# A recurrence with weight conversion beside it: one list of conversions becomes two, with a start step each

## The chip, the cores and the metric

The kernel runs on one core of a Trainium2 chip. The metric is device time in microseconds (us). The core has five engines that run side by side, each through its own instructions in a fixed order: PE (matrix products and transposes; its weight loads are shown as PEld), DVE (vector operations), ACT (scalar operations, copies out of PSUM, lookups), POOL (vector operations on SBUF) and SP (here the issue of nearly all DMAs). An instruction that waits holds up all that stand behind it on its engine.

## The reference, cut to what matters

Three parts follow one another. All data are float32; B = 4 batches, H = 8 heads, S = 768 steps of time, D = 40.

```python
# 1. recurrence: one 40 x 40 state per batch and head
for t in range(S):
    y[:, :, t] = einsum('bhd,bhde->bhe', r_t, state)
    Sa = einsum('bhde,bhe->bhd', state, a_t)
    state = state * w_t[:, :, None, :] - outer(Sa, b_t) + outer(v_t, k_t)
x = y.transpose(0, 2, 1, 3).reshape(B, S, 320)
# 2. gated layer: w_in 320 x 1024, w_out 1024 x 320
h = maximum(x @ w_in, 0)
conv = 3-tap convolution of h over time, weights conv_w per column
x = (h * sigmoid(conv)) @ w_out
# 3. Fourier transform over time and columns, norm, second layer: w_ch1, w_ch2
u = x + real(fft(fft(x, axis=1), axis=2))
out = u + maximum(norm(u) @ w_ch1, 0) @ w_ch2
```

The weights and conv_w reach the kernel as 64-bit floating-point numbers, seen as pairs of 32-bit integers.

## The kernel before, in words

**The recurrence in chunks.** Time is cut into 12 chunks of 64 steps. A block is one chunk of one batch, so there are 48 blocks, and `Attn.run` (L542) works through them in steps: step n handles block n first of all, and the three blocks ahead of it in later stages. `step` (L470) lists the stages, each ended by a yield, seven in a full step: `stage_u` (PE products from the chunk's inverse, then ACT's scaling at L390), `stage_s` (the state's increment: PE, DVE's mask at L414 and L418, POOL's addition and decay at L419 and L420), `stage_y` (the output: PE at L442 and L445 with gt, which DVE made), `stage_ut`, `stage_h` (the next chunk's right-hand side from the state), `stage_g` (PE at L428, then DVE makes gt at L432) and `stage_o` (transposes, DVE's xo at L463, the store). Early and late steps have fewer yields: steps 45 and 46 have six and five.

**Work for later blocks.** `ahead` (L526) prepares blocks 15 to 17 steps before they are used: loads, decays (scans on DVE, products such as L161 on POOL), the gram products at L203 and transposes at L239 on PE. It has nothing left to do from step 33 on. Each group of eight blocks needs the inverse of its triangular matrices. `inverse` (L292) makes it on DVE in 60 operations that depend on one another (L317 and L320) and some transposes, and then merges the parts with 256 small matmuls on PE (L344, L357) and copies on ACT. The inversion of the last group begins about step 33 and has to be merged by step 40.

**The conversion beside it.** Products on PE take the weights as float32 split into a rounded high part and a remainder. `prep` (L684) turns the 64-bit numbers into these in pieces: 12 of w_in, 16 of w_out, 15 of w_ch1 and 20 of w_ch2, in this order, in one list `self.pieces`. A piece is a load of `raw` (issued by SP at L719), two ACT operations (L729, L730), two on DVE (L732, L734), an integer addition on POOL (L736), four empty yields, and a DVE operation that joins the parts (L739). w_out needs the result alone, one store; the other weights are then rounded on ACT (L703) and subtracted on DVE (L706), with two stores. Each part ends with a yield: 8 calls for a piece of w_out, 9 for one of the others, and 1 more for the first load. All the DVE operations of it write or read the tile `pm`. Converted weights lie in DRAM until they are loaded for use. `conv_w` (L710) converts the convolution's weights, 9 calls.

`body` (L1323) gives `att.run` a chain of `prep` down to `NLEFT = 33` pieces left (all of w_in and w_out and two pieces of w_ch1) and `conv_w`: 264 calls. At each yield of a step `run` adds `SIDE = 1.2` to a counter and makes a call for each whole unit. The instructions of a call are placed, on ACT and DVE, behind the last marked instruction of the recurrence (`issue_after`, with `self.mark` and `self.markd`); other than that the order on each engine, SP's too, is made by a scheduler that takes, in program order, what is ready by its own clock. The 33 pieces left are converted later, beside the gated layer.

**The handover.** When the recurrence's instructions are all placed, the gated layer loads its weights (`moe1_start`, L767: w_in by L752 to L756, w_out by L764) and the first x (L789 to L791), which ACT and POOL split at L792 to L797. Its first product with w_in is `hp` at L655; its first with w_out is `acc` at L848, three units later. SBUF tiles of the two parts share room: the conversion's tiles (raw twice, pm twice, py twice, wh, wl: 2 x 2048 + 2 x 1024 + 2 x 1024 + 1024 + 1024 = 10,240 bytes a partition) stand at the right-hand end, where w_out's tile (8 x 320 x 4 = 10,240 bytes) is put next, and a load waits for the last use of what it overwrites.

Of the kernel before, what the change touches and what calls it, by code (L numbers as in the profile page):

```python
# [33 lines left out]
ND = 1  # L34
NF = 1
NLEFT = 33
W1P = 2
W2P = 5
L4 = 2
# [24 lines left out]
GS = 1  # L64
MG = 1
RI = 0.8
SIDE = 1.2
NA = 7
OT = 0
LG = 15  # L70
# [10 lines left out]
class Attn:  # L81
# [457 lines left out]
            self.gram_x(*divmod(m, B))  # L539
            yield  # L540

    def run(self, side):  # L542
        nc, tc = self.nc, self.tc
        self.start()
        wm = self.pst("warm")
        for _ in range(WARM):
            nc.tensor.matmul(wm[:, 0:396], self.ends[:, 0:128], self.ends, start=True, stop=True)
        self.load_pre(0, 0)
        nc.sync.dma_start(self.mdiag, self.i["mdiag"])
        self.load_pre(0, 1)  # L550
        nc.sync.dma_start(self.mltq, self.i["mlt"])
        nc.sync.dma_start(self.ident, self.i["ident"])
        self.load_pre(1, 0)
        self.grp_start(0)
        self.decay(0, 0)
        for hb in range(2):
            if hb:
                self.decay(0, 1)
            for bl in range(2):
                self.gram(0, 2 * hb + bl)  # L560
        for hb in range(2):
            self.load_v(0, hb)
        self.pads()
        for hb in range(2):
            self.load_z(0, hb)
            self.load_r(0, hb)
        inv = self.inverse(0)
        for n in range(ST0):
            next(inv)
        for hb in range(2):  # L570
            for bl in range(2):
                self.gram_x(0, 2 * hb + bl)
        with tc.issue_after(self.late.ins):
            for hb in range(2):
                self.squares(0, hb)
                if hb == 0:
                    self.load_pre(1, 1)
        self.grp_start(1)

        def half(hb):  # L580
            if hb < ST2:
                self.decay(1, hb)
            else:
                with tc.issue_after(self.first.ins):
                    self.decay(1, hb)
            self.squares(1, hb)
            for bl in range(2):
                self.gram(1, 2 * hb + bl)
                self.gram_x(1, 2 * hb + bl)
        half(0)  # L590
        for b in range(B):
            self.stage_h(0, b)
        if ST1:
            half(1)
        next(inv)
        next(inv)
        tr = self.last
        for _ in inv:
            pass
        if not ST1:  # L600
            half(1)
        live, g = [], 1
        for hb in range(2):
            self.load_v(1, hb)
        for k in range(8 - LD, 8 - LG, 2):
            h = divmod((k + LD) // 2, 2)
            self.load_pre(*h)
            with tc.issue_after(tr.ins):
                self.decay(*h)
            self.squares(*h)  # L610
        sd, na = 0.0, 8 - LG
        for n in range(B * NCH + 4):
            while live and n == live[0]["end"]:
                for _ in live.pop(0)["inv"]:
                    pass
            while g <= NCH // 2 and na + LG >= 8 * g and len(live) < 2:
                end = 8 * g - 8 if g > 1 else 4
                live.append(dict(inv=self.inverse(g), end=end, last=0, acc=0.0,
                                 rate=RI * (35 if g == 1 else 70) / 7 / max(1, end - n - MG)))
                next(live[-1]["inv"])  # L620
                g += 1
            pre = []
            for _ in range(1 + (n < NA)):
                if na <= n:
                    pre.append(self.ahead(na))
                    na += 1
            pre = itertools.chain(*pre)
            ag = -GS
            for _ in self.step(n):
                sd += SIDE  # L630
                while sd > 0:
                    with ExitStack() as st:
                        for m in [self.mark, self.markd][:1 + SM]:
                            if m is not None:
                                st.enter_context(self.tc.issue_after(m.ins))
                        next(side, None)
                    sd -= 1.0
                ag += 1.0
                if ag > 0:
                    next(pre, None)  # L640
                for k, v in enumerate(live):
                    v["acc"] += v["rate"]
                    while v["acc"] > 0 and not (v["last"] == "t" and k or v["last"] == "merge" and n < v["end"] - MG):
                        v["last"] = next(v["inv"], None)
                        v["acc"] -= 1.0
            for _ in pre:
                pass
        for _ in side:
            pass


def passes(nc, out, ops):
# [14 lines left out]
class Moe:  # L667
# [382 lines left out]
    def load_w1(self, pool):  # L1050
        w, q = FF2 // W1P, len(self.w1)
        self.w1.append(self.k320(pool, f"w_ch1_{q}", w))
        self.load_k320(self.w1[q], "w_ch1", slice(w * q, w * q + w))
# [6 lines left out]
    def moe2_rest(self, pool):  # L1060
        for _ in range(1, W1P):
            self.load_w1(pool)
        for _ in range(1, W2P):
            self.load_w2(pool)
        self.rows = pool.tile([128, 3 * B], I32, name="rows")
        self.nc.sync.dma_start(self.rows, self.i["rows"])

    def moe2(self, tp):
# [4 lines left out]
        def g3(i):  # L1073
            b, hf, f = units[i]
            q, r = divmod(f, NF2 // W1P)
            fs = slice(128 * r, 128 * r + 128)
# [246 lines left out]
def body(tc, ins, out):  # L1323
    nc = tc.nc
    with tc.tile_pool(name="dram", bufs=1, space=DRAM) as dr, tc.tile_pool(name="flag", bufs=1) as fp:
        xd = dr.tile([B, NG * P3, S], F32, name="xd")

        xh = [dr.tile([B, NG * P3, (NCH // 2 + 1) * C], F32, name=f"xd{hf}") for hf in range(2)]
        flag = fp.tile([1, 1], I32, name="flag")
        moe = Moe(tc, ins, out)  # L1330
        with ExitStack() as ctx:
            tp = ctx.enter_context(tc.tile_pool(name="prep", bufs=1, side="right"))
            att = Attn(ctx, tc, ins, [(xh[0], 0), (xh[1], NCH // 2 - 1)])
            moe.prep_start(dr, fp)
            att.run(itertools.chain(moe.prep(tp, NLEFT), moe.conv_w(tp)))
            att.in_range(flag)
        moe.run([(xh[0], 0), (xh[1], (NCH // 2 - 1) * C)])
        ok = nc.values_load(flag, min_val=0, max_val=1)
        with tc.If(ok < 1):
            General(tc, ins, xd).run()  # L1340
            moe.run([(xd, 0)] * 2)
# [21 lines left out]
```

## Time and profile before

| | |
|---|---|
| median of 3 runs | 995.05 us (995.01 to 995.82) |
| profiled execution, its own time | 997.03 us |
| its span, first to last instruction | 995.3 us |
| mean granted TensorE clock | 0.937 of full speed |
| PE busy | 906.7 us, 91% |
| DVE busy | 684.1 us, 69% |
| ACT busy | 520.7 us, 52% |
| POOL busy | 456.5 us, 46% |

Busy time is what an engine spent in instructions; matmuls are pipelined, so a busy PE is not PE at its peak. The granted clock is the share of TensorE's full 2.4 GHz that the chip allowed; its lower level is 1.2 GHz. Shares over the whole span mix stages with different limits, and the change lies in one of them, the recurrence, which fills the first half of the span; so the rows further down are by stretch.

### The profile page before, as it was taken

Reading aid. Unit: us, or ns where it says so; the run is one execution under the profiler, and the core shown is the slowest. Engines: PE = TensorE matmul, PEld = TensorE weight load, DVE = VectorE, ACT = ScalarE, POOL = GpSimd, SP = SyncE. Lnnn points to the kernel's source line nnn. Section 1 sums busy time; section 2 is a strip of 40 time slices with the busy share of each in tenths; the row PEclk is TensorE's granted clock in tenths of the full one; section 3 lists DMA queues with packets and bytes.
Section 4 is the critical chain, followed back from the end, with each engine's and each line's share of the span. In section 5 each row is a group of like instructions: output and inputs, shape, how many; then the busy total and the mean of one; then the engine's idle time right before and its main releaser. Section 6 shows DMA issues by size and latency. Waiting matters only on the chain. (4 is left out here: it accounts for less than half of the span.)

```text
span 995.3 us, 21859 instructions
## 1 busy us (share of the span) xinstructions
PE 906.7 (91%) x8178; PEld 818.7 (82%) x8178; DVE 684.1 (69%) x1322; ACT 520.7 (52%) x1448; POOL 456.5 (46%) x528
## 2 busy tenths in 40 slices
PE   5568698999989999999999699989999999999997
PEld 3557587888878888998888587777879999999997
DVE  8895997997996996881278697879684535424321
ACT  5668387676766577334376566567464431212211
POOL 6575375665665464343168566765562121101000
PEclk8667599997997999999999899998999999999999
DMA  9624346565555364339344643112105000000000
GB/s 224 178 77 128 90 126 178 154 161 147 150 138 152 98 169 114 87 98 255 81 126 134 187 141 114 54 50 70 41 1 172 20 1 21 20 20 21 20 14 31
DMA packets 102878, 101.15 MB, mean 102 GB/s; under 512 B 47160, under 2 KB 89003, under 8 KB 102763
## 3 DMA queue, kind: packets, MB, share of 16 engines
q1 hardware_dynamic: 100795, 94.73, 34.3%
q0 software_dynamic: 1968, 4.93, 1.6%
q8 instruction: 67, 1.10, 0.5%
q14 instruction: 48, 0.39, 0.2%
HBM read 74.81 MB, written 20.76 MB: 96 GB/s over the span
## 5 line engine op out<-in xcount | busy, mean ns | idle before, releaser
L831 DVE SCALAR_TENSOR_TENSOR c<-h,cw,c 128x384 f32<-128x384 f32 x128 | 113.3, 890 | 21.0 <-ACT c L829 17.4
L1085 DVE SCALAR_TENSOR_TENSOR gl<-hp,gh 128x384 fp32r<-128x384 f32 x80 | 44.4, 557 | 111.3 <-ACT gh L1084 111.2
L848 PE MATMUL acc<-w_out_f,z 128*128 128x320 f32 x384 | 118.0, 446 | 2.8 <-POOL z L837 1.1
L1084 ACT ACTIVATE gh<-hp 128x384 fp32r<-128x384 f32 x80 | 39.3, 492 | 149.8 <-PE hp L655 149.6
L848 PEld LDWEIGHTS acc<-w_out_f,z 128*128 128x128 f32 x384 | 73.5, 196 | 27.0 <-ACT x L853 1.8
L655 PE MATMUL hp<-xh,w_in_h 128*128 128x386 f32 x192 | 76.3, 397 | 14.3 <-ACT h L822 14.3
L655 PE MATMUL hp<-uh,w_ch_h 128*128 128x384 f32 x240 | 82.3, 343 | 0.0
L655 PE MATMUL hp<-ul,w_ch_h 128*128 128x384 f32 x240 | 81.0, 337 | 0.0
L1108 POOL DMA_INDIRECT out<-o,rows x12 | 11.7, 978 | 150.8 <-DVE o L1103 131.9
L317 DVE TENSOR_TENSOR tmp<-A 128x30 f32<-128x30 f32 (+9 forms) x150 | 77.1, 514 | 3.3
L320 DVE TENSOR_TENSOR A<-A,tmp 128x30 f32<-128x30 f32 (+9 forms) x150 | 76.8, 512 | 3.5
L203 PE MATMUL gram<-abd,kb 120*128 120x192 f32 (+1 forms) x288 | 64.6, 371 | 13.4 <-DMA w<-in_w 6.9
L419 POOL TENSOR_TENSOR st<-st,sm 120x360 f32<-120x360 f32 x40 | 48.3, 1208 | 56.9 <-DVE sm L418 53.0
L1098 PE MATMUL acc<-w_ch_h,gh 128*128 128x320 f32 x240 | 73.2, 312 | 0.0
L1098 PE MATMUL acc<-w_ch_l,gh 128*128 128x320 f32 x240 | 73.0, 309 | 0.0
L203 PEld LDWEIGHTS gram<-abd,kb 120*128 120x128 f32 x288 | 56.0, 227 | 17.3 <-POOL lk L223 9.7
L655 PE MATMUL hp<-xl,w_in_h 128*128 128x386 f32 x192 | 67.1, 349 | 0.0
L736 POOL TENSOR_TENSOR pm<-pm,py 128x160 int32<-128x160 int32 (+2 forms) x64 | 45.0, 703 | 44.0 <-DVE pm L734 17.1
L832 ACT ACTIVATE c<-c 128x384 f32<-128x384 f32 x64 | 33.4, 522 | 60.5 <-DVE c L831 60.3
L161 POOL TENSOR_TENSOR kb<-kb,vx 120x768 f32<-120x768 f32 x24 | 44.0, 1833 | 45.5 <-DMA kb<-in_kb 25.3
L445 PE MATMUL yp<-x,gt 128*64 128x40 f32 x768 | 54.8, 233 | 10.1 <-DVE gt L432 10.1
L445 PEld LDWEIGHTS yp<-x,gt 128*64 128x64 f32 x768 | 51.0, 143 | 13.2 <-DVE gt L432 11.9
(226 smaller groups left out, 2585.9 us busy)
## 6 DMA issues: line engine op xcount, KB each, us to landing
kb<-in_kb SPq DMA_DIRECT2D x24, 360.0 KB
vbd<-in_vbd SPq DMA_DIRECT2D x24, 320.0 KB
xd<-xo SPq DMA_DIRECT2D x56, 90.0 KB
w<-in_w SPq DMA_DIRECT2D x24, 185.6 KB
a<-in_a SPq DMA_DIRECT2D x24, 180.0 KB
z<-in_zv SPq DMA_DIRECT2D x24, 180.0 KB
zt<-in_vt SPq DMA_DIRECT2D x24, 180.0 KB
rbd<-in_r SPq DMA_DIRECT2D x72, 60.0 KB
```

Source lines behind the costliest of these rows:

```text
L161: self.markp = nc.gpsimd.tensor_tensor(kb, kb, vx[:, :, 2:66].unsqueeze(2).to_broadcast([P3, 6, 2, C]), op=ALU.mult)
L203: nc.tensor.matmul(gp[:, 192 * gi:192 * gi + 64 * nh], d["kb"][:, bl * NG + gi].rearrange("p a b -> p (a b)"), abd[:, 0:nh, bl * NG + gi], ...
L317: nc.vector.tensor_tensor(tmp, A[:, s + 1:32, s:s + 1].to_broadcast([128, n, s]), A[:, s:s + 1, 0:s].to_broadcast([128, n, s]), op=ALU.mult)
L320: nc.vector.tensor_tensor(A[:, s + 1:32, 0:s], A[:, s + 1:32, 0:s], tmp, op=ALU.add)
L419: nc.gpsimd.tensor_tensor(self.st[b], self.st[b], t, op=ALU.add)
L445: nc.tensor.matmul(yp[0:64, D * h:D * h + D], gt[:, h], d["x"][:, bl, D * h:D * h + D], start=(c == 0), stop=True, skip_group_check=True)
L655: nc.tensor.matmul(out, l, r, start=(j == 0), stop=(j == len(ops) - 1))
L736: nc.gpsimd.tensor_tensor(m, m, y, op=ALU.add)
L831: nc.vector.scalar_tensor_tensor(c, h[:, j:HS + j], cw[:, f, j:j + 1], c, op0=ALU.mult, op1=ALU.add)
L848: nc.tensor.matmul(self.acc[t][:, 0:DM], z[:, ts], w[:, f], start=(f == 0), stop=(f == NF1 - 1))
L1085: nc.vector.scalar_tensor_tensor(gl, hp[:, 0:HS], 0.0, gh.bitcast(F32), op0=ALU.max, op1=ALU.subtract)
L1098: nc.tensor.matmul(self.acc[t][:, 0:DM], l[:, ts], r, start=(f == 0 and j == 0), stop=(f == NF2 - 1 and j == 2))
```

## The change

The chain handed to `run` becomes two lists, each with the step from which it is taken. The first starts at step `N1ST = 4` and stops at `NLEFT + NW = 49` pieces left: it holds the 12 pieces of w_in, two of w_out, and then conv_w. The second starts at step `N2ND = 38` and goes down to 33 pieces left: 14 of w_out and two of w_ch1. `SIDE` becomes a pair: no calls before step 4, 1.2 for each yield from step 4, 2.2 from step 38. A call goes to the first list that isn't at its end. What is not done when the steps are over is still placed behind them. The pieces, their instructions and their order are as before, and so is the conversion beside the gated layer.

```diff
+NW = 16
+N1ST, N2ND = 4, 38
...
-SIDE = 1.2
+SIDE = (1.2, 2.2)
...
-    def run(self, side):
+    def run(self, sides):
...
+            k = sum(n >= m for m, _ in sides) - 1
             for _ in self.step(n):
-                sd += SIDE
+                sd += SIDE[k] if k >= 0 else 0.0
                 while sd > 0:
                     with ExitStack() as st:
                         for m in [self.mark, self.markd][:1 + SM]:
                             if m is not None:
                                 st.enter_context(self.tc.issue_after(m.ins))
-                        next(side, None)
+                        for _, side in sides[:k + 1]:
+                            if next(side, self) is not self:
+                                break
                     sd -= 1.0
...
-        for _ in side:
-            pass
+        for _, side in sides:
+            for _ in side:
+                pass
...
-            att.run(itertools.chain(moe.prep(tp, NLEFT), moe.conv_w(tp)))
+            att.run([(N1ST, itertools.chain(moe.prep(tp, NLEFT + NW), moe.conv_w(tp))), (N2ND, moe.prep(tp, NLEFT))])
```

## Rows read from the trace of the kernel before

**Rows 1.** The page, section 4: the chain that ended last, by engine.

```profile
PE 31%; DVE 8%; ACT 3%; issue 2%; DMA 1%; POOL 1%; DVEq 0%; ACTq 0%; POOLq 0%
```

**Rows 2.** Stretches (start:end, length): busy of PE, PEld, DVE, ACT, POOL; clock; DMA; GB/s.

```profile
62.20:118.10 55.90, 40.55 (x622) 37.29 (x622) 42.64 (x82) 35.55 (x117) 27.41 (x30) 0.71 0.39 109
118.10:274.20 156.10, 146.92 (x1715) 131.18 (x1714) 138.87 (x270) 112.33 (x358) 97.46 (x103) 0.93 0.55 148
274.20:393.10 118.90, 110.27 (x1395) 98.42 (x1393) 100.94 (x208) 76.87 (x242) 68.61 (x82) 0.93 0.52 140
393.10:449.80 56.70, 56.40 (x794) 51.38 (x794) 44.48 (x96) 23.80 (x65) 18.89 (x25) 1.00 0.34 88
449.80:497.60 47.80, 47.24 (x507) 42.28 (x505) 10.96 (x27) 17.77 (x49) 11.09 (x16) 1.00 0.62 168
```

**Rows 3.** The same stretches, instructions on tile pm alone: DVE, ACT, POOL.

```profile
62.20:118.10 55.90, 6.07 (x11) 2.13 (x5) 2.19 (x3) 0.71 0.39 109
118.10:274.20 156.10, 26.40 (x54) 10.38 (x26) 11.53 (x15) 0.93 0.55 148
274.20:393.10 118.90, 17.97 (x43) 5.04 (x14) 7.71 (x13) 0.93 0.52 140
393.10:449.80 56.70, 0.00 (x0) 0.00 (x0) 0.00 (x0) 1.00 0.34 88
```

**Rows 4.** Single lines L390, L719, L714: duration min/median/max ns, first and last start.

```profile
L390 ACT ACTIVATE z<-u x48: 424/433/434, 62.2 to 488.7; 64x320 f32<-64x320 f32 x48
L719 SPq DMA_DIRECT2D raw<-in_w_out x16: 364/383/1528, 209.2 to 354.9; - x16
L714 DVE COPY cw<-pm x1: 178/178/178, 389.3 to 389.3; 128x24 f32<-128x24 f32 x1
```

**Rows 5.** Waits, 274.2 to 393.1: who for whom, us in total, times, longest.

```profile
PE yp L445 <- DVE gt L432: 6.7, 5, 2.4
DVE pm L739 <- POOL pm L736: 1.5, 3, 0.9
```

**Rows 6.** Stretches, PE's instructions on tile kb (two rows), then on tile bp.

```profile
274.20:393.10 118.90, 17.87 (x100) 0.93 0.52 140
393.10:449.80 56.70, 1.35 (x9) 1.00 0.34 88
...
393.10:449.80 56.70, 2.21 (x128) 1.00 0.34 88
```

**Rows 7.** Timeline: start, duration, engine, line, operation, tiles, count; last inversion, step 40.

```profile
440.28 3.66 DVE L330 STREAM_TRANSPOSE tt<-A 128x1024 f32<-128x1024 f32 x2
...
449.80 0.42 ACT L390 ACTIVATE z<-u 64x320 f32<-64x320 f32 x1
```

**Rows 8.** Timeline about 460 us: gt made, and used by y.

```profile
458.84 0.69 DVE L432 TENSOR_TENSOR gt<-gp,mlt 128x512 f32<-128x512 f32 x1 [3.62 <-PE gp L428]
...
461.40 1.08 PE L445 MATMUL yp<-x,gt 128*64 128x40 f32 x16
```

**Rows 9.** Timeline about 326 us: POOL's product and the inversion on DVE.

```profile
325.35 1.72 POOL L161 TENSOR_TENSOR kb<-kb,vx 120x768 f32<-120x768 f32 x1 [1.80 <-DVE tmp L317]
325.56 1.64 DVE L317 TENSOR_TENSOR tmp<-A 128x108 f32<-128x108 f32 x1
...
327.54 0.30 DVE L317 TENSOR_TENSOR tmp<-A 128x130 f32<-128x130 f32 x1
```

**Rows 10.** The handover: lines L764 and L848; timeline of xf's casts and first hp.

```profile
L764 SPq DMA_DIRECT2D w_out_f<-w_out_h x1: 647/647/647, 452.9 to 452.9; - x1
L848 PE MATMUL acc<-w_out_f,z x384: 430/432/741, 505.7 to 748.0; 128*128 128x320 f32 x192
...
469.31 0.83 ACT L792 CAST xh<-xf 128x772 fp32r<-128x772 f32 x1 [2.41 <-DMA xf<-xd]
470.22 1.82 POOL L795 TENSOR_TENSOR xl<-xf,xh 128x772 fp32r<-128x772 f32 x1 [1.36 <-ACT xh L792]
...
497.61 0.44 PE L655 MATMUL hp<-xh,w_in_h 128*128 128x386 f32 x1
```

## The prediction

> **What bounds the kernel now.** I read the page's digits first, then the chain of waits, then a table of busy time by stretch, then who waited for whom in the stretches that the change touches. The profiled execution took 997.03 us, 1.7 us more than its 995.3 us span, and stands 2.0 us above the median of 995.05 us. I make the sum against the execution and take the difference over to the median as it is.
>
> The chain of waits is of no help here. Its shares add up to 46% of the span [rows 1], so, followed back from the last instruction, it reaches only to about 537 us and breaks off there. The recurrence, where the whole change lies, ends near 497 us. So I cut the recurrence into stretches by its steps. A step's mark is the scaling of u on ACT at L390, one for each of the 48 blocks, from 62.2 to 488.7 us [rows 4]; the starts of steps 0, 4, 20, 32 and 40 give the five stretches of [rows 2].
>
> They show two regimes. In steps 4 to 19 (156.1 us, 9.8 us a step) and 20 to 31 (118.9 us, 9.9 us a step) DVE is busy for 89% and 85%, PE for 94% and 93% at a mean granted clock of 0.93 [rows 2]. In steps 32 to 39 (56.7 us, 7.1 us a step) and 40 to 47 PE is busy nearly throughout at full clock, and DVE falls to 44.5 of 56.7 and 11.0 of 47.8 us [rows 2]. Two kinds of work fill the early steps and are missing from the late ones: the preparation of later blocks (grams, decays), and the weight conversion. The conversion's instructions on DVE all read the tile pm. They take 6.1, 26.4 and 18.0 us in the first three stretches and nothing after 393.1 us [rows 3]; the last, the copy of conv_w, starts at 389.3 us [rows 4]. This fits the code's pace: 264 calls at 1.2 per yield and seven yields a step are 31.4 steps.
>
> So in the early steps DVE has too much to do, and it shows on PE: in steps 20 to 31 PE stood idle 8.6 us, of which 6.7 us were waits of y's matmuls for gt, which DVE makes [rows 2, 5]. The late steps are PE's. The change carries DVE work from the one regime to the other.
>
> **Where the pieces go.** The first list now holds 14 pieces and conv_w: 1 + 12 x 9 + 2 x 8 + 9 = 134 calls, which at 8.4 a step last 16 steps, 4 to 19. The second holds 14 pieces of w_out and 2 of w_ch1: 1 + 14 x 8 + 2 x 9 = 131 calls at 15.4 a step. Steps 38 to 44 make 49 yields, or 108 calls; step 45 makes six yields and step 46 five. The last w_out store is call 113, in step 45; the last w_ch1 store is call 131, at the end of step 46. Steps 0 to 3 and 20 to 37 get no conversion.
>
> **Steps 20 to 31: a gain.** DVE loses 17.97 us and the 1.5 us that it waited for POOL's add ahead of L739 [rows 3, 5]: 118.9 - 19.5 = 99.4 us, if every microsecond of it counted. PE sets another floor. Steps 32 to 39 take 56.7 us with PE busy 56.4; in them stand one merge and one prepared block. The merge's first half costs 2.2 us, and I take its second half, with as many matmuls, as equal: 4.4. The gram and transpose of kb are 1.4 us there for 9 matmuls, the count of one block [rows 6]. A bare step is then (56.7 - 4.4 - 1.4) / 8 = 6.4 us. Steps 20 to 31 need 12 x 6.4 + 2 merges x 4.4 + 100 / 9, or 11, blocks x 1.4 = 101 us on PE. So the stretch cannot go below 101, a gain of 18. DVE would then have 83 us of 101, 82%; steps 32 to 39 run at PE's floor with 78%. Against the full gain: late in each group DVE itself sits and waits for the next group's grams, and the inversion's 60 dependent operations don't speed up. I take **13**. The low end is half of PE's 8.6 us of idle time, 4.3; a loss is excluded, since every engine there only loses work.
>
> The clock is part of it. Its mean is 0.93 in this stretch and 1.00 in all that follow [rows 2], so the lower of the two levels, 1.2 GHz, holds for 14% of it, some 17 us, and these bring up to 8 us of the 18 if PE no longer idles there.
>
> **Steps 0 to 3: a small gain.** 6.1 us of DVE work go, out of 42.6 busy in 55.9 us [rows 2, 3], and with them the raw loads that run beside the start's other loads. Much of this stretch is latency of the first inversions; I take **2** between 0 and 6.1.
>
> **Steps 4 to 19: about the same.** The rate is as before, but there are 12 pieces of w_in, with two DVE operations on top of L732's and L734's, where the tail of this stretch had w_out. 15 pieces cost 26.4 us now [rows 3]; 14 and conv_w, two more of them w_in, make about 28. I take a loss of **1** between 0 and 2.
>
> **Steps 38 to 46: a loss.** 18 us over 13 conversions (conv_w among them) is 1.4 us each on DVE [rows 3], so 16 pieces bring 22 us, 11 us of ACT work and 9 of POOL. Two places differ.
> In steps 38 and 39 the last group's inversion still runs: its transposes end at 443.9, and step 40's u follows the merge at 449.8 [rows 7]. The inversion is a chain that DVE's 12 us of idle time in steps 32 to 39 [rows 2] cannot shorten, and 30 calls, 3.7 pieces, come in beside its end: up to 5 us, of which I take 2.5, since about half of them will be issued behind its last operations.
> From step 40 DVE has 37 us idle [rows 2] for the other 12 pieces, 17 us. What can hurt there is an order, not an amount: a DVE operation that waits for POOL's add holds gt behind it. PE needs gt at 461.40, when DVE has been done with it since 459.53 [rows 8], so a delay of up to 1.9 us a step is free. I take 1 us for the eight steps. Behind the waiting operation also stand sm, which POOL and the next step's h wait for, with more room than gt, and xo. Together **3.5**, from 0 to 22.
>
> Here the Trainium skill has a rule that speaks against the change. First the row: an L317 product that ran beside POOL's add to kb took 1.64 us, the next and larger one 0.30 [rows 9]. The page "SBUF — State Buffer", section "Who interferes with whom", says that a VectorE instruction with two SBUF inputs and a GpSimd instruction that reads SBUF exclude each other for a whole instruction. By that rule each POOL add of the conversion (7.71 us for 13) also holds up an inversion operation in steps 38 and 39, 3.7 x 0.6 = 2.2 us on top; the sum would be 2 us less of a gain.
>
> **The handover: little.** w_out's tile takes, byte for byte, the room of the conversion's tiles (both are 10,240 bytes a partition at the right-hand end). Now its load is issued at 452.9 and first used at 505.7 [rows 10]. After the change it has to wait for call 131 and its store. By the old clock that is about 491 us; 1.31 MB at the 168 GB/s of that stretch [rows 2] are 7.8 us, so it lands near 499, 6.7 us ahead of its use. I take **0.5** between 0 and 7. The stores and raw loads on SP (16 loads, 18 stores) stand between the loads of the last blocks; in steps 0 to 31 they stood so too. The 3.9 MB they carry beside the 8 MB of that stretch are within what the queues move at times, but not free.
>
> **Sum.** 13 + 2 - 1 - 3.5 - 0.5 = 10.0 us. The execution would take 987.0, the median 995.05 - 10.0 = **985.0 us**.
>
> **Rivals.**
> *All of it comes through* (0.17): steps 20 to 31 go to PE's floor, the start gives 4, the tail costs nothing: 18 + 4 - 1 = 21, so 974. For it: PE ran at its floor in steps 32 to 39 with as dense a DVE. Against: the inversion's latency.
> *PE is the bound already* (0.12): only 4.3 come back in steps 20 to 31 and 1 at the start, 4.3 + 1 - 1 - 3.5 - 0.5 = 0.3, so 994.7. For it: PE is busy for 93% there. Against: 17 us of that stretch ran at the lower clock, and a bare step needs 6.4 us of PE, not 9.9.
> *The handover is late* (0.10): SP holds w_out's load, which waits until 491, ahead of the first xf load, which ACT now splits at 469.3. Then xf queues behind 1.31 MB and lands near 499, and after ACT's and POOL's casts (0.83 and 1.82 us, and two smaller ones behind the latter) the first hp matmul, now at 497.6 [rows 10], is some 7 us late: gain 3, so 992. Against: SP's order puts ready loads ahead of earlier work that is not ready, as the late blocks' loads stand behind w_in's.
> *The tail pays* (0.13), the case on the other side: PE has no idle time in the last ten steps, so each DVE delay of gt beyond 1.9 us in a step is lost in full. If none of the 22 us is hidden, the sum is 15.5 - 2 - 22 = -8.5 and the time 1003.5; it is slower than before once more than 13.5 of the 22, 61%, comes through. For it: L739 waited for POOL three times in steps 20 to 31 [rows 5], and the pace is 1.8 times as high against steps that are a third shorter. Against: 37 us of idle DVE.
> *The order does not move* (0.03): the instructions are placed as before; 995.
>
> **How the numbers follow.** The forecast has 0.45. A change below 0.2%, 2 us, cannot be told from none. Faster takes the forecast, the first rival, most of the handover and a third of the PE case: 0.76. Within 0.2%: 0.09. Slower: the tail and a little of the PE case: 0.15. The forecast's own range is 979 to 991; the range that holds 8 in 10 runs from the first rival's end, 974, to 997, where it takes in the PE case and the lower part of the tail's.
>
> **What would show it.** Right: no pm instruction between step 20 and step 37; steps 20 to 31 in 103 to 109 us at a clock near 1; steps 38 and 39 some 2 us longer; steps 40 to 47 within 2 us of 47.8; w_out's load issued near the end of the recurrence and the first acc matmul still 8 us behind the first hp matmul. Wrong: steps 20 to 31 still above 114 us; PE idle before y's matmuls in steps 40 to 47; the first hp matmul waiting for xf, or acc for a DMA.

## The result and the profile after

The changed kernel is slower. Its median is 1010.18 us (1004.56 to 1012.21, 6 runs), against 996.77 us (995.01 to 1001.97, 6 runs) for the kernel before beside it: a ratio of 1.0101, with a 95% interval of 1.0067 to 1.0135. The forecast was 985.0 us, the range 974 to 997. The profiled execution took 1012.18 us, its span 1010.4 us, 15.1 us more than before. From here on, lines of attention code stand two further down than before (L390 is L392), those of the gated layer seven (L655 is L662, L764 is L771).

The first view is the table by stretch, as [rows 2], cut at the same steps (their u marks are now at 61.7, 115.9, 278.4, 388.3 and 445.4). The last two rows are the end of the recurrence and the handover. Columns: start:end, length, busy us of PE, PEld, DVE, ACT and POOL, granted clock, DMA share, GB/s.

```profile
61.70:115.90 54.20, 40.51 (x622) 36.68 (x622) 44.47 (x81) 34.89 (x115) 26.76 (x29) 0.75 0.38 108
115.90:278.40 162.50, 151.48 (x1706) 135.47 (x1706) 140.65 (x268) 110.45 (x352) 94.25 (x102) 0.89 0.50 139
278.40:388.30 109.90, 103.24 (x1403) 92.13 (x1402) 85.41 (x161) 69.59 (x217) 59.38 (x68) 1.00 0.46 120
388.30:445.40 57.10, 56.41 (x793) 51.30 (x793) 45.36 (x99) 24.30 (x68) 19.20 (x26) 1.00 0.35 89
445.40:495.00 49.60, 47.62 (x508) 42.10 (x505) 25.09 (x71) 26.95 (x80) 19.28 (x31) 1.00 0.58 156
495.00:520.00 25.00, 11.26 (x44) 10.20 (x44) 3.90 (x9) 7.12 (x13) 5.24 (x9) 0.59 0.77 236
```

Two rows stand out. Steps 20 to 31 fell from 118.9 to 109.9 us, as the change meant. And in the 25 us after the recurrence PE is busy for 11.3 us at a clock of 0.59, where the kernel before had PE busy for 21.7 of the 22.4 us from 497.6 to 520, at 1.00.

The same table for the conversion alone (tile pm; DVE, ACT, POOL) answers to [rows 3]. The work did move: none is left in steps 20 to 31, and DVE has 16.7 us of it after step 40.

```profile
278.40:388.30 109.90, 0.00 (x0) 0.00 (x0) 0.00 (x0) 1.00 0.46 120
388.30:445.40 57.10, 2.10 (x3) 0.35 (x1) 0.52 (x1) 1.00 0.35 89
445.40:499.00 53.60, 16.71 (x47) 6.23 (x17) 8.38 (x15) 0.97 0.60 160
```

What PE waits for in the gap is in the waits between 490 and 520 us (who for whom: us in total, times, longest):

```profile
PE hp L662 <- DMA w_in_h<-w_in_h: 9.7, 1, 9.7
PE hp L662 <- DMA w_in_l<-w_in_l: 3.5, 1, 3.5
```

It is not w_out, and not x either (the first x is split by 462.2 us). It is w_in, the first weight of the gated layer. PE's timeline (start, duration, tiles, idle time before), first in the kernel before, then after the change, shows both waits, and matmuls at 0.53 us where those of the kernel before took 0.34:

```profile
497.17 0.39 PE L460 MATMUL yt<-ident,ys 64*120 64x64 f32 x3 [0.56 <-ACT ys L448]
...
498.24 0.34 PE L655 MATMUL hp<-xh,w_in_h 128*128 128x386 f32 x1
```

```profile
494.64 0.39 PE L462 MATMUL yt<-ident,ys 64*120 64x64 f32 x3 [0.56 <-ACT ys L450]
504.83 0.69 PE L662 MATMUL hp<-xh,w_in_h 128*128 128x386 f32 x1 [9.68 <-DMA w_in_h<-w_in_h]
505.31 0.53 PE L662 MATMUL hp<-xl,w_in_h 128*128 128x386 f32 x1
...
509.99 0.69 PE L662 MATMUL hp<-xh,w_in_l 128*128 128x386 f32 x1 [3.51 <-DMA w_in_l<-w_in_l]
```

And SP's timeline shows why w_in is late: its loads are issued only when the last conversion has been stored, 51 us later than before. First the single line of w_in's first load in the kernel before, then SP after the change:

```profile
L752 SPq DMA_DIRECT2D w_in_h<-w_in_h x2: 363/610/856, 449.3 to 449.7; - x2
```

```profile
498.16 0.33 SPq L711 DMA_DIRECT2D w_ch_h<-wh  x1
498.96 0.33 SPq L714 DMA_DIRECT2D w_ch_l<-wl  x1
499.38 0.38 SPq L726 DMA_DIRECT2D raw<-in_w_ch  x1
500.70 0.80 SPq L759 DMA_DIRECT2D w_in_h<-w_in_h  x2
501.67 0.45 SPq L760 DMA_DIRECT2D w_in_h<-w_in_h  x1
...
502.81 1.10 SPq L763 DMA_DIRECT2D w_in_l<-w_in_l  x2
503.94 0.49 SPq L771 DMA_DIRECT2D w_out_f<-w_out_h  x1
```

The 15.1 us of the span, added up: the recurrence ends 2.5 us earlier (last yt 494.8 instead of 497.3); the gap from there to the first hp grows from 0.3 to 10.0 us, +9.7; and from the first hp to the end it takes 505.6 us instead of 497.7, +7.9. Of these 7.9, 3.5 are the second wait, for w_in_l. About 3.7 are the clock: the 22 hp matmuls that start between 504.8 and 515.9 take 11.1 - 3.5 = 7.6 us, and at the full-clock pace of 0.175 us they would take 3.9. The other 0.7 us are not accounted for.

### The profile page after: what moved, and what is told of

It is laid out like the page before. It is cut to its first block, busy times and chain, and to the rows that moved or that the text cites. A ratio compares the mean times of both kernels' runs of the same rounds, so it can differ in the third digit from the quotient of the medians.

```text
span 1010.4 us, 21846 instructions
## 1 busy us (share of the span) xinstructions
PE 907.3 (90%) x8178; PEld 816.8 (81%) x8178; DVE 688.6 (68%) x1322; ACT 520.5 (52%) x1448; POOL 448.6 (44%) x528
## 5 line engine op out<-in xcount | busy, mean ns | idle before, releaser
L662 PE MATMUL hp<-xh,w_in_h 128*128 128x386 f32 x192 | 77.9, 406 | 23.6 <-ACT h L829 13.9
L322 DVE TENSOR_TENSOR A<-A,tmp 128x30 f32<-128x30 f32 (+9 forms) x150 | 81.1, 541 | 3.5
L662 PE MATMUL hp<-uh,w_ch_h 128*128 128x384 f32 x240 | 82.3, 343 | 0.0
L662 PE MATMUL hp<-ul,w_ch_h 128*128 128x384 f32 x240 | 81.0, 337 | 0.0
L319 DVE TENSOR_TENSOR tmp<-A 128x30 f32<-128x30 f32 (+9 forms) x150 | 73.5, 490 | 3.4
L205 PEld LDWEIGHTS gram<-abd,kb 120*128 120x128 f32 x288 | 53.5, 218 | 19.4 <-issue 13.3
L662 PE MATMUL hp<-xl,w_in_h 128*128 128x386 f32 x192 | 68.5, 357 | 0.0
L421 POOL TENSOR_TENSOR st<-st,sm 120x360 f32<-120x360 f32 x40 | 44.7, 1116 | 47.2 <-DVE sm L420 45.2
L447 PE MATMUL yp<-x,gt 128*64 128x40 f32 x768 | 54.2, 231 | 10.2 <-DVE gt L434 10.1
L662 PEld LDWEIGHTS hp<-xh,w_in_h 128*128 128x128 f32 x192 | 38.0, 198 | 31.1 <-ACT h L829 17.6
L1105 PE MATMUL acc<-w_ch_h,gl 128*128 128x320 f32 x240 | 61.4, 309 | 0.0
```

The source lines that it names most:

```text
L205: nc.tensor.matmul(gp[:, 192 * gi:192 * gi + 64 * nh], d["kb"][:, bl * NG + gi].rearrange("p a b -> p (a b)"), abd[:, 0:nh, bl * NG + gi], ...
L319: nc.vector.tensor_tensor(tmp, A[:, s + 1:32, s:s + 1].to_broadcast([128, n, s]), A[:, s:s + 1, 0:s].to_broadcast([128, n, s]), op=ALU.mult)
L322: nc.vector.tensor_tensor(A[:, s + 1:32, 0:s], A[:, s + 1:32, 0:s], tmp, op=ALU.add)
L421: nc.gpsimd.tensor_tensor(self.st[b], self.st[b], t, op=ALU.add)
L447: nc.tensor.matmul(yp[0:64, D * h:D * h + D], gt[:, h], d["x"][:, bl, D * h:D * h + D], start=(c == 0), stop=True, skip_group_check=True)
L662: nc.tensor.matmul(out, l, r, start=(j == 0), stop=(j == len(ops) - 1))
```

## The experiments

Where the tiles lie can be read off the addresses of the built programs; no trace shows them. In bytes per partition, right-hand end at 229,344:

```
conversion (raw, pm, py, wh, wl)      219,104 to 229,344
gated layer, pool "b_w", before and after:
  w_out_f                             198,624 to 208,864
  w_in_l (2 parts)                    208,864 to 217,056
  w_in_h (3 parts)                    217,056 to 229,344
```

So the tiles of that pool are stacked towards the right-hand end with the last one at the end: it is w_in's high parts that lie on the conversion's room, and w_out lies clear of it.

**The theory (room)** is that w_in's loads wait for the conversion's room, so that the end of the last conversion, however small, sets the start of the gated layer. The rivals put the loss elsewhere: on the conversions' work and traffic in the recurrence's last steps (load), on w_out's own late data (w_out), or on the start at step 4. Below, a gain is measured against the kernel before, run beside them on the same chip (median 998.11 us for the first four experiments, 997.17 for the last four).

### Room taken away: the conversion's pool moved to the other end of SBUF

```diff
-            tp = ctx.enter_context(tc.tile_pool(name="prep", bufs=1, side="right"))
+            tp = ctx.enter_context(tc.tile_pool(name="prep", bufs=1))
```

> The changed kernel, with the conversion's tiles in SBUF room that nothing of the gated layer's weights takes (left-hand end in place of the right-hand end). Theory 'room': w_in's load waited because its room was held by the conversion; here it is issued near 445 us, w_out's alone waits for its data, the first hp matmul follows the recurrence's last transpose at once (near 495), the execution comes out some 2 to 3 us below the kernel before (ratio 0.997). Rival 'load' (the conversion's work and traffic beside the last ten steps are what delays the gated layer): first hp still near 505, ratio 1.010 as in the changed kernel. Rival 'w_out' (w_out's own late data is what costs): first hp early, first acc still near 520, ratio 1.010.

Measured: 990.27 us (986.88 to 997.54, 12 runs), ratio 0.9934 [0.9905, 0.9964]. The conversions stand in the last steps as before; only their room differs. w_in is issued at 441.5, right at step 40's start (441.2), and hp no longer waits for it. The single line of w_in's first load, then the first hp on PE:

```profile
L759 SPq DMA_DIRECT2D w_in_h<-w_in_h x2: 362/392/421, 441.5 to 442.0; - x2
```

```profile
490.39 0.57 PE L462 MATMUL yt<-ident,ys 64*120 64x64 f32 x3 [1.55 <-ACT ys L450]
490.89 0.19 PE L524 MATMUL rp<-ro,rs 120*1 120x1 f32 x2
491.01 0.69 PE L662 MATMUL hp<-xh,w_in_h 128*128 128x386 f32 x1
```

One word of placement turns +1.0% into -0.7%, more than the -0.3% that I expected. The same conversions in the last steps, the same start and a w_out issued only at 492.8 are all still there, so none of the rivals is the cause of the loss.

### w_out put on the conversion's room instead of w_in

```diff
+                with tc.tile_pool(name="b_wo", bufs=1, reuse_waits="tile", side="right") as op, \
+                        tc.tile_pool(name="b_w", bufs=1, reuse_waits="tile", side="right") as wp, \
...
-                        self.moe1_start(wp)
+                        self.moe1_start(wp, op)
...
-        self.wo = [wp.tile([128, NF1, DM], F32, name="w_out_f")]
+        self.wo = [op.tile([128, NF1, DM], F32, name="w_out_f")]
```

> The changed kernel, with w_out's tile in a pool of its own, which takes exactly the conversion's room, and w_in in room that comes free at step 40: the layout that the prediction had assumed. Theory 'room': w_in's load near 445, first hp near 495; w_out's load after the last conversion, near 500, landing 5 to 8 us later, first acc near 508 in place of 503: 4 to 5 us more than the run with the room on the left, ratio 1.002. Rival 'load': 1.010. Rival 'w_out': 1.010, first acc near 520.

This is the layout that the prediction believed in: w_out in a pool of its own at the right-hand end, at 219,104 to 229,344, and w_in below it. Measured: 987.81 us (985.66 to 996.45, 12 runs), ratio 0.9916 [0.9885, 0.9947], by its median the fastest kernel of this study, and faster than both kernels of the case. The steps 4 to 19 and 20 to 31 as in [rows 2], the single lines of the first loads of w_in and of w_out, and PE at the handover:

```profile
115.60:267.70 152.10, 140.59 (x1709) 125.82 (x1708) 137.22 (x267) 110.91 (x352) 95.59 (x102) 0.97 0.53 149
267.70:377.90 110.20, 105.87 (x1401) 94.71 (x1398) 85.69 (x162) 69.55 (x217) 59.38 (x68) 0.97 0.45 119
```

```profile
L759 SPq DMA_DIRECT2D w_in_h<-w_in_h x2: 363/392/421, 435.4 to 435.8; - x2
L771 SPq DMA_DIRECT2D w_out_f<-w_out_h x1: 370/370/370, 498.1 to 498.1; - x1
```

```profile
486.63 0.39 PE L462 MATMUL yt<-ident,ys 64*120 64x64 f32 x3 [0.56 <-ACT ys L450]
486.95 0.19 PE L524 MATMUL rp<-ro,rs 120*1 120x1 f32 x2
487.07 0.49 PE L662 MATMUL hp<-xh,w_in_h 128*128 128x386 f32 x1
...
504.27 6.70 PE L855 MATMUL acc<-w_out_f,z 128*128 128x320 f32 x24 [1.56 <-DMA w_out_f<-w_out_h]
```

Now it is w_out that waits for the conversion: it is issued at 498.1, and the first acc stands 17.2 us behind the first hp, where 8.1 were usual. That costs nothing in the end: from the first hp to the end it takes 497.6 us, before 497.7. PE has other units' hp to do, waits 1.56 us, and then does 24 acc matmuls in a row. My expectation put a price on this lateness and was wrong by about 1%.

### The amount: nine calls and 24 columns at the last step

```diff
-N1ST, N2ND = 4, 38
+N1ST, N2ND = 0, 47
...
-SIDE = (1.2, 2.2)
+SIDE = (1.2, 1.2)
...
-            att.run([(N1ST, itertools.chain(moe.prep(tp, NLEFT + NW), moe.conv_w(tp))), (N2ND, moe.prep(tp, NLEFT))])
+            att.run([(0, moe.prep(tp, NLEFT)), (N2ND, moe.conv_w(tp))])
```

> The kernel before in all but one thing: the conversion of conv_w, 9 calls with 24 columns, is put off to step 47; all of w_in, w_out and the two pieces of w_ch1 are converted from step 0 on as before. Theory 'room': the small conversion holds the room to the end, w_in's load is issued near 497 in place of 449, first hp near 501 with a second wait for w_in's low part, 8 to 12 us more, ratio 1.010. Rivals 'load' and 'w_out': nothing heavy has moved, ratio 1.000.

This is the order of the kernel before, all pieces from step 0 at 1.2, except for the conversion of conv_w, 24 columns, at step 47. Measured: 1007.02 us (1002.4 to 1013.83, 6 runs), ratio 1.0111 [1.0058, 1.0164], as much as the whole change costs. DVE's two operations of it, of 0.17 us each, then SP, then PE:

```profile
495.40 0.17 DVE L746 SCALAR_TENSOR_TENSOR pm<-raw,pm 128x24 int32<-128x24 int32 x1
...
495.76 0.17 DVE L721 COPY cw<-pm 128x24 f32<-128x24 f32 x1
```

```profile
496.36 0.87 SPq L759 DMA_DIRECT2D w_in_h<-w_in_h  x2
```

```profile
501.04 0.69 PE L662 MATMUL hp<-xh,w_in_h 128*128 128x386 f32 x1 [3.31 <-DMA w_in_h<-w_in_h]
...
506.22 0.69 PE L662 MATMUL hp<-xh,w_in_l 128*128 128x386 f32 x1 [3.53 <-DMA w_in_l<-w_in_l]
```

The recurrence is as long as before (last yt at 497.4, before 497.3); w_in is issued 0.4 us behind the copy of conv_w, 47 us later than before, and the whole loss lies behind that. When the room comes free decides, not how much work holds it.

### The start: the first list from step 0

```diff
-N1ST, N2ND = 4, 38
+N1ST, N2ND = 0, 38
```

> The changed kernel with its first list begun at step 0 in place of 4; the second still at step 38. The handover is as in the changed kernel, so all theories expect a ratio near 1.010; if putting off the start matters by itself (in the traces steps 4 to 19 were 6 us longer after the change, steps 0 to 3 about 2 us shorter), this one comes out some 4 us below the changed kernel, ratio 1.006; if those 6 us are chance of the execution, within 2 us of it.

Measured: 1007.42 us (1005.71 to 1010.14, 8 runs), ratio 1.0102 [1.0066, 1.0139]. The same as the change, so the start at step 4 has no part in the loss. w_in is issued at 499.6 and the first hp comes at 502.7.

### The control: the second layout with the order of before

To the kernel before, with its one list from step 0, only w_out's own pool is given.

```diff
-        self.wo = [wp.tile([128, NF1, DM], F32, name="w_out_f")]
+        self.wo = [op.tile([128, NF1, DM], F32, name="w_out_f")]
```

> The kernel before (one list from step 0), with w_out's tile in a pool of its own as in the split run. Control for the layout alone. Theory 'room': with the conversion done at step 31 no room is held, w_in's load still waits for the last inversion near 449 us: no change, ratio 1.000. Rival 'layout' (the split run's gain comes from the layout of the pools and not from the lists): 0.992.

Measured: 996.51 us (993.13 to 1002.64, 12 runs), ratio 0.9995 [0.9971, 1.0018]. The layout alone brings nothing: w_out is now issued at 391.6, but w_in, at 448.5, and the first hp, at 497.2, stay where they were. So the 0.84% of the kernel with w_out on the conversion's room belong to the change of order, once the layout lets it through.

```profile
L759 SPq DMA_DIRECT2D w_in_h<-w_in_h x2: 362/502/641, 448.5 to 448.9; - x2
```

### The two halves of the change in the second layout

```diff
 # both with w_out's own pool; first kernel:
-N1ST, N2ND = 4, 38
+N1ST, N2ND = 0, 38
 # second kernel:
-            att.run([(N1ST, itertools.chain(moe.prep(tp, NLEFT + NW), moe.conv_w(tp))), (N2ND, moe.prep(tp, NLEFT))])
+            att.run([(N1ST, itertools.chain(moe.prep(tp, NLEFT), moe.conv_w(tp)))])
```

> The split run with its first list begun at step 0: the late second list alone, with w_in's room free. If steps 20 to 31 bring nearly all of the gain (9 us of DVE relief less a tail of 1 to 4 us), ratio 0.994, some 2 us above the split run, the 2 us that steps 0 to 3 lose again. If the start step is worth more, nearer 0.998.

> One list as before, begun at step 4, with the split layout: the start step alone. The conversion then ends near step 35, in steps where PE is the bound. Steps 0 to 3 give 2 us; steps 32 to 35 take conversions that had stood in steps 28 to 31 and lose DVE room that is nearly full (44.5 of 56.7 us): between a gain of 2 and a loss of 2 us, ratio 0.998 to 1.002.

The late second list alone: 992.97 us (991.24 to 996.33, 9 runs), ratio 0.9946 [0.9923, 0.9968]. The start at step 4 alone: 994.87 us (990.38 to 1001.85, 12 runs), ratio 0.9972 [0.9946, 0.9998]. Their product is 0.9918, and both together measured 0.9916: about two thirds of the gain are the late list's. The part of the start is hardly told apart from none, and I had expected none (0.998 to 1.002).

### Only the addresses swapped, in the same pool

```diff
-        self.wo = [wp.tile([128, NF1, DM], F32, name="w_out_f")]
         self.wi = self.k320(wp, "w_in", FF1)
+        self.wo = [wp.tile([128, NF1, DM], F32, name="w_out_f")]
```

> The changed kernel, with the two lines swapped that make the tiles of w_out and w_in, inside the one pool: w_in's tiles then lie in room that is free at step 40, w_out's in the conversion's. If the wait is for each tile's own room, this equals the split run, 0.992. If the whole pool opens only when all of its room is free, the order of the loads stays as in the changed kernel and the ratio 1.010, with w_in's load near 500.

The changed kernel, with w_in's tiles put ahead of w_out's. w_out's tile now lies on the conversion's room, and w_in's stand at 198,624 to 219,104, the same place as in the fastest kernel. Measured: 1007.27 us (1003.58 to 1010.4, 6 runs), ratio 1.008 [1.0053, 1.0107]. By address w_in was free to go, but it wasn't loaded any earlier:

```profile
L759 SPq DMA_DIRECT2D w_in_h<-w_in_h x2: 323/378/432, 499.9 to 500.2; - x2
```

This corrects the theory. The wait isn't that of a tile for what lies beneath it alone: in this run all loads into the pool come after the last use of the room that the pool as a whole takes over. With a pool of its own for w_out, w_in's load no longer waits for the conversion (435.4). Which rule of the allocator or the scheduler makes it so is not shown.

## Why the prediction was wrong

**The step that failed is the handover**, in the sentence "w_out's tile takes, byte for byte, the room of the conversion's tiles". The two sizes are equal, and I took the equality for the place; the section on the handover ahead of the prediction has the same mistake. The pool's first tile stands at its low end, so w_in's high parts, made last, stand on the conversion's room; and even with w_out there, w_in's load waits if it is in the same pool (the swap). The rule that I went by, that a load waits for the last use of what it overwrites, was too narrow. So the load that was put off is the one that the first product of the gated layer needs, and not one with 8 us of slack [rows 10]. I had 0.5 us for the handover, 0 to 7; it was 9.7 + 7.9 = 17.6. The medians agree: from 0.9934 with the conversion's room elsewhere to 1.0101 are 1.7%, some 17 us.

That a load has to wait for call 131 and its store was right. "About 491" for that store was early: it is at 498.96. I had 3.7 pieces done in steps 38 and 39; one was. The 15 others took from 446.8 to 499.0 us, 3.5 us each, so the 2.7 that were missing are, as an estimate, some 9 us. The first piece, taken up by ACT at step 38, got no further before the last inversion was off DVE, 11 us later. ACT's timeline, then DVE's:

```profile
426.78 0.35 ACT L736 ACTIVATE pm<-raw 128x160 f32<-128x160 f32 x1
```

```profile
433.86 3.66 DVE L332 STREAM_TRANSPOSE tt<-A 128x1024 f32<-128x1024 f32 x2
...
437.64 1.04 DVE L739 TENSOR_SCALAR pm<-pm 128x160 f32<-128x160 f32 x1
```

That wait alone does not explain it. With the first list from step 0, DVE starts on the first piece at 431.6, ahead of the inversion's transposes, and still the second is taken up only after step 40's mark and the last store comes as late, at 498.3. What holds the second piece back stays open.

With w_in on the room, a store at 491 would, as an estimate from these times (498.96 - 491), have spared some 8 us of the 17.6, not all.

The terms of the sum, one execution against one (a gain is positive; the first mark, 61.7 instead of 62.2, gives 0.5 more):

| step of the sum | forecast | measured | worked out from |
|---|---|---|---|
| steps 20 to 31 | +13 (4.3 to 18) | +9.0 | 118.9 to 109.9 |
| steps 0 to 3 | +2 | +1.7 | 55.9 to 54.2 |
| steps 4 to 19 | -1 (0 to -2) | -6.4 | 156.1 to 162.5 |
| steps 38 and 39 | -2.5 | 0 | 19.1 in both |
| steps 32 to 37 | 0 | -0.4 | 37.6 to 38.0 |
| step 40 to last yt | -1 | -1.9 | 47.5 to 49.4 |
| handover | -0.5 | -17.6 | 0.3 to 10.0, 497.7 to 505.6 |
| sum | +10.0 | -15.6 | |

**Steps 20 to 31** came out as forecast in kind: nothing of pm is left, the clock is 1.00, and DVE's busy time fell from 100.9 to 85.4 us. The size is 9 rather than 13. The stretch is 109.4 and 110.2 us long in the first two experiments, and 113.8 and 112.1 with the late list alone. PE still waits for gt there, 5.6 us where it was 6.7 [rows 5], so the conversion had little part in making gt late. That the inversion on DVE does it is likely, but not shown.

```profile
PE yp L447 <- DVE gt L434: 5.6, 6, 1.3
```

**The tail** was the rival on the slower side, at up to 22 us. It cost 1.9 here, 2.0 in the first experiment (47.5 to 49.5) and 4.0 in the second (51.5), so the forecast of 3.5 holds as a sum, but not in its parts. Steps 38 and 39 take 19.1 us in all ten kernels. Here the inversion is off DVE before the first conversion gets on; with the first list from step 0 two conversion operations (431.6 and 432.2) and POOL's addition (432.6) come ahead of its transposes, which end at 438.9, and the length is still 19.1. I had taken these steps for the inversion's; they look like PE's, which is busy for 56.4 of the 57.1 us of steps 32 to 39. But one piece with 2.1 us on DVE came in there and not 3.7 with 5, so my price for the full load was not put to the test. The rule of the Trainium skill that I weighed there ("SBUF — State Buffer", section "Who interferes with whom") had nothing to act on, since no addition of the conversion on POOL stood beside an operation of the inversion; no run here tests it. The row that I read it beside has POOL's product with kb, not an addition.

**Steps 0 to 3** gave what I expected, for a partly wrong reason: 6.3 us of the conversion on DVE still stand there, from 77.6 us on, although no call is made before step 4; the scheduler has put them ahead. The gain can't come from less work on DVE.

**Steps 4 to 19** took 6.4 us longer, where I had 1. DVE's busy time went up by 1.8 us and the conversion's part of it hardly moved (25.7 for 26.4). What moved is PE: 1706 matmuls take 151.5 us at a clock of 0.89, in the second experiment 1709 take 140.6 at 0.97, with the same order of the lists. The stretch goes with the clock from one execution to the next: 152.1 us at 0.97, 156.1 and 156.5 at 0.93 (before, and the first list from step 0), 162.5 at 0.89. Why the clock is granted so differently there stays open. Three kernels that start at step 4 had 0.88 or 0.89 (the change, the start alone in the second layout, the swap), but the first experiment with 0.92 and the fastest kernel start there too. It isn't what made the change slower: the first experiment has 158.9 us in this stretch and gains 0.7%, and the first list from step 0 has 156.5 and loses as much as the change.

So with the handover repaired the rest of the forecast stands: 985.0 us was a ratio of 0.990 to 995.05, and the layout that I had in mind measured 0.9916 [0.9885, 0.9947]. That it agrees so well is partly luck: in its profiled execution steps 20 to 31 gave 8.7 us and not 13, and 4.0 came from steps 4 to 19, the stretch that goes with the clock, where I had a loss of 1.

## What to carry to other kernels

Before work is put off to the end of a stage, ask who gets its memory next and when that is first used: here nine calls on 24 columns at the last step cost as much as 16 pieces, because what counts is the last use of the room. Equal sizes prove no place: read the addresses in the built program, and see which loads of the next stage are issued right after the old tiles' last use. Where old and new must share room, let the new tile that is needed last take it, in a pool of its own.

## What the runs showed of the hardware that was not expected

In PE's idle time and after it the granted clock is 0.53 and then 0.50, the level of 1.2 GHz, up to 510 us, and it is back at 1.00 from 520 on (columns: PE busy, clock, DMA share, GB/s). Before it, PE was busy for 47.6 of 49.6 us at 1.00. The waits of 13.2 us, with the 3.7 us that the slow matmuls took longer, come to some 17.

```profile
495.00:505.00 10.00, 0.32 (x4) 0.53 0.83 241
505.00:510.00 5.00, 1.49 (x5) 0.50 0.94 292
510.00:520.00 10.00, 9.45 (x37) 0.70 0.61 204
520.00:540.00 20.00, 19.69 (x89) 1.00 0.35 107
```

That the wait made the clock fall is not shown. In the first two experiments hp waits for no load, and its first matmuls take 0.53 us as well, only for less long. The same columns from about the first hp on, in the kernel before, in the first experiment and in the second:

```profile
497.60:510.00 12.40, 11.70 (x61) 1.00 0.45 125
...
491.00:504.00 13.00, 12.44 (x54) 0.79 0.90 281
...
487.00:500.00 13.00, 11.99 (x59) 0.87 0.68 190
```

Loads that nothing holds up still take long when several come at once: w_in's high parts, issued from 500.7 on, are first used at 504.8, and w_in_l, issued at 502.8, at 510.0, while the DMA engines moved 292 GB/s in the last 5 us.
